# Forgetting attention with an FFN on one core: GpSimd scales the early exponentials and makes gl from the first group on

## The chip, the core and the metric

The kernel runs on one core of a Trainium2 chip. A core has five engines with an instruction queue each: TensorE (in the profile PE for matmuls and PEld for weight loads), VectorE (DVE), ScalarE (ACT), GpSimd (POOL) and SyncE (SP), which here only issues DMAs. Each works through its queue in order, and waits on semaphores where it needs another's result. The metric is the device time of one execution in microseconds. Before the change it is 1215.92 us, the median of three runs (1212.28 to 1219.12).

## The reference

Eight batches of eight heads, 576 tokens, head size 64. Attention has a forget gate: the logarithms of f are summed up along the sequence, and the difference of the sums at query and key is added to the scores. The result, 4608 tokens by 512, goes through an FFN with 2048 hidden units and a leaky ReLU.

```python
scores = scale * np.matmul(q, k.transpose(0, 1, 3, 2))
cum = np.cumsum(np.log(np.clip(f, 0.0001, 1.0)), axis=-1)
decay = cum[:, :, :, None] - cum[:, :, None, :]
scores = np.where(causal, -1000000000.0, scores + decay)
scores = scores - np.max(scores, axis=-1, keepdims=True)
attn = np.exp(scores)
attn = attn / (np.sum(attn, axis=-1, keepdims=True) + 1e-09)
x = np.matmul(attn, v)            # then rearranged to (4608, 512)
h = x @ w_in
g = np.maximum(0.01 * h, h)
out = g @ w_out
```

## The kernel before

**High and low halves.** The FFN's matmuls work on fp32r, in which a float32 is kept as a high half and a low half: x as xh and xl, the weights as win_h, win_l, wout_h, wout_l, the activations g as gh and gl. A product is the sum of three matmuls (high by high, high by low, low by high). The low half is always made by a subtraction, gl = g - gh.

**Early phase.** For the first three batches (NE = 3) the first 256 tokens are computed separately, two heads at a time: twelve steps, called pairs here. A pair (b, g) goes through

- `early_load`: DMAs of q, k (tile qk) and v (tile ve), issued by SP;
- `early_scores` (L254): score matmuls on TensorE (sce), eviction with mask and running extreme on DVE into four tiles ze (two of 128 x 128, two of 128 x 256; L279), exponentials on ACT with their sums into sume (L283), sume plus a small number and its reciprocal on DVE (L288, L289), and the scaling of the four ze by it (L291);
- `early_values`, one pair later: transposes of ze on TensorE (tre), their copies on ACT (pte, L303), the product with v (ave), and from it xh on ACT (L316) and xl on DVE (L317) for the FFN groups 0 and 1, or a copy xe that goes to DRAM (L312) for the third batch.

Between these, `weights` prepares sixteen pieces of weights (eight of w_in, eight of w_out, in turn): a DMA of 1 MB into one of two raw buffers (wraw), then two steps on ACT (wt at L170, the high half at L172) and five on DVE (L171, L173, L175, L179, and the low half at L180). All pieces go through one buffer wt.

**FFN.** `ffn` is a generator. A group is 256 tokens; a slice p of a group is 256 of the 2048 hidden units. For each slice TensorE makes h from 24 matmuls, ACT makes g (L587), DVE the high half gh (L590), and DVE or GpSimd the low half gl (L592). The second product (`second`, into o) of a slice is emitted one slice later, 24 matmuls. `fill(n)` takes n quanta of this generator; FQ says how many after each early pair (4 after the fifth, 8 after the sixth, then 8 after each).

**Main loop.** `for t in range(nt + 1)` (L675) works through 64 heads and pulls FFN quanta between their pieces; in its last round, t = nt, no new head is loaded. After it the FFN's rest is drained. In this loop GpSimd has work of its own: low halves of q and k (tiles s, m), of v (fixed_vs), of the groups' inputs (xs), and small copies. Before the loop it fills the fixed tiles (`fix`).

**Who makes gl.** `heads[0]` is False until the main loop begins, True for t < nt, and False again from t = nt on. Where it is True, GpSimd makes gl, else DVE. In the trace 111 are on GpSimd and 33 on DVE.

**Order.** The program is written in the order above, but a scheduler arranges the instructions anew by when it thinks that each can run, and fixes an order for each engine. So a change on one engine also moves instructions on others. A few matmuls on a tile of zeros (warm) stand among the early pairs to keep TensorE active.

Of the kernel before, what the change touches and what calls it, by code (L numbers as in the profile page):

```python
# [12 lines left out]
AF = mybir.ActivationFunctionType  # L13
ALU = mybir.AluOpType
# [23 lines left out]
def forgetting_attention_ffn(ctx, tc, qT, kT, v4, vr, f, w_in, w_out, out):  # L38
# [6 lines left out]
    nc = tc.nc  # L45
# [23 lines left out]
    def width(i):  # L69
        return min((i + 1) * P, S)  # L70
# [32 lines left out]
    def matmul(*args, **kw):  # L103
        work[0] += 1
        nc.tensor.matmul(*args, **kw)  # L105
# [7 lines left out]
    def warm(n):  # L113

        ps = psum.tile([P, 512], F32, tag="h", name=f"warm_{len(warmed)}")
        warmed.append(n)
        for _ in range(n):
            matmul(ps, still[:, :P], still, start=True, stop=True)
# [92 lines left out]
    for i in range(NCH):  # L211
        c = slice(i * P, width(i))
# [12 lines left out]
    def load(t):  # L225

        s, c0, c1 = tasks[t]
        h = state[t] = {}
        a, n = c0 * P, S
        for name, src, lo in (("q", qT, a), ("k", kT, 0)):  # L230
            x = h[name] = one.tile([P, S], F32, tag=f"{name}raw", name=f"{name}raw_{t}")
            for o in range(2):
                nc.sync.dma_start(x[o * D:(o + 1) * D, lo:n], src[s][:, lo:n])
        if s % 2 == 0:
            g = s // 2
            vm = fixed["vm"]
            nc.sync.dma_start(vm[:, :, :NFULL], v4[g])
            nc.sync.dma_start(vm[:REST, :, NFULL], vr[g])
            pairs[s // 2, c0] = {}
# [14 lines left out]
    def early_scores(b, g):  # L254
        e = early[b, g]
        mx = one.tile([P, 4], F32, tag="max", name=f"maxe_{b}_{g}", bufs=3)
        sm = one.tile([P, 4], F32, tag="sum", name=f"sume_{b}_{g}", bufs=3)
        for i in range(2):
            n = width(i)
            ps = [  # L260
                psum.tile([P, 512], F32, tag="sc", name=f"sce_{b}_{g}_{2 * o + i}")[:, :n]
                for o in range(2)
            ]
            for o in range(2):
                x = e["qk"][o * D:(o + 1) * D]
                matmul(ps[o], x[:, 0, i * P:n], x[:, 1, :n], start=True, stop=False)
            for o in range(2):
                s = b * HPB + 2 * g + o
                matmul(
                    ps[o], pick[:, s:s + 1].broadcast_to([P, P]), decay_r[i],  # L270
                    start=False, stop=True,
                )
            for o in range(2):
                c = 2 * o + i
                tag = ZE[g % 2][c]
                z = e[c] = one.tile(
                    [P, n], F32, tag=tag, name=f"ze_{b}_{g}_{c}", bufs=BUFS.get(tag, 1)
                )
                nc.vector.tensor_tensor_reduce(  # L279
                    out=z, in0=ps[o], in1=tri[:, TRI - n:], scale=-SCALE, scalar=3.0e38,  # L280
                    op0=ALU.add, op1=ALU.min, accum_out=mx[:, c:c + 1],
                )
                nc.scalar.activation(  # L283
                    z, z, AF.Exp, bias=mx[:, c:c + 1], scale=-1.0, accum_out=sm[:, c:c + 1]
                )
            if b * HPB // 2 + g < WARM[2]:
                warm(WARM[1])
        nc.vector.tensor_scalar(sm, sm, 1.0e-9, None, op0=ALU.add)  # L288
        nc.vector.reciprocal(sm, sm)  # L289
        for c in range(4):  # L290
            nc.scalar.activation(e[c], e[c], AF.Copy, scale=sm[:, c:c + 1])  # L291

    def early_values(b, g):
        e = early[b, g]
# [236 lines left out]
    def spans(t):  # L531
        a, n = tasks[t][1] * P, S
        return [(a, n)] if n - a <= 512 else [(a + P, n), (a, a + P)]

    groups, staged = {}, {}
    since, done = {}, []
# [7 lines left out]
    def fetch_group(n):  # L544
        if n not in groups and n not in staged and (n + 1) * T <= ready[0]:
            xs = staged[n] = one.tile([P, NCC, T], F32R, tag="b4", name=f"xs_{n}", bufs=B4)
            since[n] = work[0]
            nc.sync.dma_start(xs.bitcast(F32), xd[:, n * T:(n + 1) * T].rearrange("(c p) t -> p c t", p=P))
# [8 lines left out]
    def ffn():  # L557
        pending = None
        half = NFC // 2
        order = [(0, 0, HP), (1, 0, HP), (0, HP, half), (1, HP, half)]  # L560
        order += [(n, 0, half) for n in range(2, NG)]
        for at, (n, p0, p1) in enumerate(order):
            while (n + 1) * T > ready[0]:
                yield False
            if n not in groups:
                if n not in staged:
                    fetch_group(n)
                while n not in groups:
                    yield False
            acc = [None, None]  # L570
            for p in range(p0, p1):
                while len(loaded) < 2 * (p + 1):
                    yield False
                xh, xl = groups[n]
                ph = psum.tile([P, 2, T], F32, tag="h", name=f"h_{n}_{p}")
                for e in range(2):
                    fs = slice(e * P, (e + 1) * P)
                    for c in range(NCC):
                        for x, (w, xx) in enumerate(((win_h[p], xh), (win_h[p], xl), (win_l[p], xh))):
                            matmul(  # L580
                                ph[:, e, :], w[:, c, fs], xx[:, c, :],
                                start=(c == 0 and x == 0), stop=(c == NCC - 1 and x == 2),
                            )
                    if e == 0:
                        yield True
                g = one.tile([P, 2, T], F32, tag="b2", name=f"g_{n}_{p}", bufs=B2)
                nc.scalar.activation(g, ph, AF.Prelu, alpha=0.01)  # L587
                gh = one.tile([P, 2, T], F32R, tag="b2", name=f"gh_{n}_{p}", bufs=B2)
                gl = one.tile([P, 2, T], F32R, tag="b2", name=f"gl_{n}_{p}", bufs=B2)
                nc.vector.tensor_copy(gh, g)  # L590
                eng = nc.gpsimd if heads[0] else nc.vector
                eng.tensor_tensor(gl, g, gh.bitcast(F32), op=ALU.subtract)  # L592
                yield True
                if pending is not None:
                    yield from second(*pending)
                if p0 < p and at + 1 < len(order):
                    fetch_group(order[at + 1][0])
                pending = (n, p, p0, p1, gh, gl, acc)
        yield from second(*pending)
# [27 lines left out]

    parts = {}
    quanta = ffn()
    heads = [False]  # L630
    ready, used, credit = [0], [0], [0.0]

    def fill(n):

        settle()
        credit[0] += n
        while credit[0] >= 1:
            credit[0] -= 1
            if not next(quanta, None):
                credit[0] = 0  # L640
                return
            used[0] += 1

    nt = len(tasks)
# [28 lines left out]
    load(0)  # L673
    split(0)
    for t in range(nt + 1):  # L675
        heads[0] = t < nt
        if t + 1 < nt:
            load(t + 1)
        before = list(range(max(tasks[t - 1][1] - 1, 0), NCH)) if t else []
        now = list(range(*tasks[t][1:])) if t < nt else []  # L680
        have = ready[0] // T * NQ - used[0]
        left = min((e + 2 - t for e in ends if e + 1 >= t), default=1)
        step = min(have / (left + SLACK), MAXQ) / 8
        fill(step)
        for i in range(5):
            if i in before:
                transposes(t - 1, i)
            if i in now:
                scores(t, i)
            fill(step)  # L690
            if i == 1 and t and tasks[t - 1][0] % 2:
                inverse(t - 1)
        if t:
            for part in range(len(spans(t - 1))):
                values(t - 1, part)
                fill(step)
            if tasks[t - 1][0] % 2:
                normalise(t - 1)
            s, c0, c1 = tasks[t - 1]
            if s % HPB == HPB - 1:  # L700
                ready[0] = place[s // HPB, c0 * P] + S - c0 * P
        if t + 1 < nt:
            split(t + 1)
        fill(step * (3 - len(spans(t - 1)) if t else 1))
# [37 lines left out]
```

## Time and profile before

| | |
|---|---|
| median of three runs | 1215.92 us |
| the profiled execution's own time | 1216.96 us |
| its span, first to last instruction | 1215.0 us |
| PE busy | 1190.4 us (98%) |
| DVE busy | 623.4 us (51%) |
| ACT busy | 628.6 us (52%) |
| POOL busy | 467.9 us (39%) |
| L291 on ACT, 48 instructions | 17.9 us, 447 ns each |
| gl on POOL, 111 | 146.9 us, 1324 ns each |
| gl on DVE, 33 | 23.3 us, 705 ns each |

The span is cut into stages: the early phase runs to about 165 us, the main loop from there to about 1110 us, and the rest is FFN alone. A share of the whole span says little here; the stages differ. In rows of single instructions the first number is the start in microseconds from the span's begin, the second the duration; then engine, line, operation, output<-input with the program's names, shapes and count. A bracket at the end gives the idle time of the engine before it and what ended it. Durations of matmuls include their pipeline, so that TensorE's pace is read from rows with many of them.

### The profile page before, as it was taken

Reading aid. Unit: us, or ns where it says so; the run is one execution under the profiler, and the core shown is the slowest. Engines: PE = TensorE matmul, PEld = TensorE weight load, DVE = VectorE, ACT = ScalarE, POOL = GpSimd, SP = SyncE. Lnnn points to the kernel's source line nnn. Section 1 sums busy time; section 2 is a strip of 40 time slices with the busy share of each in tenths; the row PEclk is TensorE's granted clock in tenths of the full one; section 3 lists DMA queues with packets and bytes.
Section 4 is the critical chain, followed back from the end, with each engine's and each line's share of the span. In section 5 each row is a group of like instructions: output and inputs, shape, how many; then the busy total and the mean of one; then the engine's idle time right before and its main releaser. Section 6 shows DMA issues by size and latency. Waiting matters only on the chain.

```text
span 1215.0 us, 22228 instructions
## 1 busy us (share of the span) xinstructions
PE 1190.4 (98%) x7812; PEld 1070.4 (88%) x7812; DVE 623.4 (51%) x1682; ACT 628.6 (52%) x1631; POOL 467.9 (39%) x475
## 2 busy tenths in 40 slices
PE   8999989999999999999999999999999999999998
PEld 5678879888889999999999999999999999999997
DVE  6898556666645555455544444545444434553211
ACT  5876546667645565555545445454444444652111
POOL 2000255564455445454344453534454544531000
PEclk9899999999999999999999999999999999999999
DMA  6554233334333233323231322222223222211000
GB/s 193 168 192 165 83 103 110 95 104 140 107 106 97 79 97 97 114 80 92 83 109 51 89 80 90 73 90 61 75 84 90 60 69 81 72 57 47 18 18 18
DMA packets 81103, 110.53 MB, mean 91 GB/s; under 512 B 19616, under 2 KB 50704, under 8 KB 80992
## 3 DMA queue, kind: packets, MB, share of 16 engines
q1 hardware_dynamic: 80992, 109.11, 29.6%
q8 instruction: 62, 1.02, 0.3%
q14 instruction: 49, 0.40, 0.1%
HBM read 82.62 MB, written 18.58 MB: 83 GB/s over the span
## 4 chain that ended last, share of the span: by engine, by line
PE 86%; DVE 4%; ACT 3%; DMA 3%; issue 2%; POOL 1%; SPq 0%; ACTq 0%; POOLq 0%; DVEq 0%
PE h L105 32%; PE o L105 30%; PE tr L109 7%; PE av L105 7%; PE sc L105 7%; PE sce L105 1%; DMA kraw<-in_kT 1%; DMA wraw<-in_w_out 1%; ACT fixed_z L384 1%; PE ave L105 1%; DVE fixed_z L378 1%; DMA wraw<-in_w_in 1%; DVE pl L430 1%; DMA xd<-x 0%; DVE wraw L179 0%
## 5 line engine op out<-in xcount | busy, mean ns | idle before, releaser
L105 PE MATMUL h<-xh,win_h 128*128 128x256 f32 x1152 | 330.2, 287 | 0.3 <-ACT xh L316 0.3
L105 PE MATMUL h<-xh,win_l 128*128 128x256 f32 x1152 | 327.9, 285 | 0.0
L105 PE MATMUL h<-xs,win_h 128*128 128x256 f32 x1024 | 290.0, 283 | 4.0 <-POOL xs L143 4.0
L592 POOL TENSOR_TENSOR gl<-g,gh 128x512 fp32r<-128x512 f32 x111 | 146.9, 1324 | 290.9 <-DVE gh L590 269.0
L105 PE MATMUL o<-wout_h,gh 128*128 128x512 f32 x576 | 230.6, 400 | 0.0
L105 PE MATMUL o<-wout_l,gh 128*128 128x512 f32 x576 | 226.6, 393 | 0.0
L105 PE MATMUL o<-wout_h,gl 128*128 128x512 f32 x576 | 225.3, 392 | 0.0
L105 PEld LDWEIGHTS h<-xh,win_h 128*128 128x128 f32 x1152 | 220.7, 192 | 3.4 <-ACT xh L316 0.8
L105 PEld LDWEIGHTS h<-xh,win_l 128*128 128x128 f32 x1152 | 221.2, 192 | 0.7 <-issue 0.7
L384 ACT ACTIVATE fixed_z<-fixed_z,max 128x192 f32<-128x192 f32 (+3 forms) x272 | 161.0, 592 | 106.0 <-DVE max L378 102.4
L378 DVE CUSTOM_DVE_ANT_0 fixed_z<-sc,tri 128x192 f32<-128x192 f32 (+3 forms) x272 | 122.6, 452 | 159.3 <-PE sc L105 156.3
L105 PEld LDWEIGHTS h<-xs,win_h 128*128 128x128 f32 x1024 | 195.6, 191 | 6.6 <-POOL xs L143 4.6
L587 ACT ACTIVATE g<-h 128x512 f32<-128x512 f32 x144 | 85.8, 596 | 217.3 <-PE h L105 212.5
L428 ACT CAST ph<-tr 128x192 fp32r<-128x192 f32 (+3 forms) x360 | 126.4, 373 | 138.5 <-PE tr L109 98.6
L590 DVE CAST gh<-g 128x512 fp32r<-128x512 f32 x144 | 72.3, 502 | 209.4 <-ACT g L587 206.7
L430 DVE TENSOR_TENSOR pl<-tr,ph 128x384 fp32r<-128x384 f32 (+3 forms) x296 | 137.8, 467 | 76.2 <-ACT ph L428 75.7
L143 POOL TENSOR_TENSOR s<-qraw,s 64x576 fp32r<-64x576 f32 (+1 forms) x64 | 78.6, 1228 | 208.5 <-ACT s L347 208.5
L109 PE MATMUL tr<-ident_r,fixed_z 128*128 128x128 f32 x888 | 145.8, 274 | 7.3 <-DVE ph L435 2.4
L109 PEld LDWEIGHTS tr<-ident_r,fixed_z 128*128 128x128 f32 x888 | 107.4, 140 | 30.0 <-ACT rbr L508 5.0
L105 PEld LDWEIGHTS o<-wout_h,gl 128*128 128x128 f32 x576 | 108.2, 188 | 24.1 <-DVE maxe L279 0.4
L105 PEld LDWEIGHTS o<-wout_h,gh 128*128 128x128 f32 x576 | 108.7, 189 | 15.6 <-issue 0.3
L105 PEld LDWEIGHTS o<-wout_l,gh 128*128 128x128 f32 x576 | 108.8, 189 | 14.7
(108 smaller groups left out, 1731.9 us busy)
## 6 DMA issues: line engine op xcount, KB each, us to landing
kraw<-in_kT SPq DMA_DIRECT2D x128, 144.0 KB
qraw<-in_qT SPq DMA_DIRECT2D x80, 144.0 KB
wraw<-in_w_in SPq DMA_DIRECT2D x16, 512.0 KB
wraw<-in_w_out SPq DMA_DIRECT2D x16, 512.0 KB
fixed_vm<-in_v SPq DMA_DIRECT2D x32, 256.0 KB
xs<-xd SPq DMA_DIRECT2D x16, 512.0 KB
out<-ost SPq DMA_DIRECT2D x28, 256.0 KB
xd<-x SPq DMA_DIRECT2D x20, 288.0 KB
```

What stands on the lines that cost most here:

```text
L105: nc.tensor.matmul(*args, **kw)
L109: nc.tensor.transpose(*args)
L143: nc.gpsimd.tensor_tensor(out, a, b, op=ALU.subtract)
L378: nc.vector.tensor_tensor_reduce(out=z[:, a:b], in0=ps[:m, :b - a], in1=tri[:m, at:at + b - a], scale=-SCALE, scalar=3.0e38 if x == 0 else ...
L384: nc.scalar.activation(z, z, AF.Exp, bias=h["max"][:m, last:last + 1], scale=-1.0, accum_out=fixed["sum" + "ab"[s // 2 % 2]][:m, i, s % 2: ...
L428: nc.scalar.copy(strided(ph, run), source(ps, run))
L430: nc.vector.tensor_tensor(strided(pl, run), source(ps, run), strided(ph, run).bitcast(F32), op=ALU.subtract)
L587: nc.scalar.activation(g, ph, AF.Prelu, alpha=0.01)
L590: nc.vector.tensor_copy(gh, g)
L592: eng.tensor_tensor(gl, g, gh.bitcast(F32), op=ALU.subtract)
```

## The change

The scaling of the early exponentials goes from ACT to GpSimd, and gl is made by GpSimd in all cases but one: DVE makes it only after the main loop has ended (`done` is filled there). So fourteen gl of the early phase and one of the round t = nt move from DVE to GpSimd. What is computed stays the same.

```diff
         for c in range(4):
-            nc.scalar.activation(e[c], e[c], AF.Copy, scale=sm[:, c:c + 1])
+            nc.gpsimd.tensor_scalar(e[c], e[c], sm[:, c:c + 1], None, op0=ALU.mult)
...
-                eng = nc.gpsimd if heads[0] else nc.vector
+                eng = nc.vector if done else nc.gpsimd
                 eng.tensor_tensor(gl, g, gh.bitcast(F32), op=ALU.subtract)
...
-    heads = [False]
...
-        heads[0] = t < nt
```

The scheduler's orders change in the early phase, and at one place near the end. In the names of the rows below, the numbers behind a tile tell the pair within a batch, the slice or the buffer apart.

On ACT, before the change, ahead of the last xh of group 0 (the row of L316 with ave_3):

```order
L316 CAST xh_172<-ave_2_462 128x256
L283 ACTIVATE ze_0_1_499,sume_0_475<-ze_0_1_499,maxe_0_474 128x256
L283 ACTIVATE ze_0_3_502,sume_0_475<-ze_0_3_502,maxe_0_474 128x256
L170 ACTIVATE wt_519<-wraw_516 128x1024
L303 COPY pte_3_0_531<-tre_3_0_527 128x384
L303 COPY pte_3_1_537<-tre_3_1_533 128x384
L291 ACTIVATE ze_0_0_482<-ze_0_0_482,sume_0_475 128x128
L291 ACTIVATE ze_0_1_499<-ze_0_1_499,sume_0_475 128x256
L291 ACTIVATE ze_0_2_485<-ze_0_2_485,sume_0_475 128x128
L291 ACTIVATE ze_0_3_502<-ze_0_3_502,sume_0_475 128x256
L172 CAST win_h_95<-wt_519 128x1024
L316 CAST xh_172<-ave_3_539 128x256
```

The same place on ACT in the changed kernel:

```order
L316 CAST xh_172<-ave_2_462 128x256
L283 ACTIVATE ze_3_1_422,sume_3_398<-ze_3_1_422,maxe_3_397 128x256
L283 ACTIVATE ze_3_3_425,sume_3_398<-ze_3_3_425,maxe_3_397 128x256
L172 CAST wout_h_110<-wt_442 128x1024
L347 CAST s_1_1806<-qraw_1746 128x320
L283 ACTIVATE ze_0_0_482,sume_0_475<-ze_0_0_482,maxe_0_474 128x128
L303 COPY pte_3_0_531<-tre_3_0_527 128x384
L303 COPY pte_3_1_537<-tre_3_1_533 128x384
L283 ACTIVATE ze_0_2_485,sume_0_475<-ze_0_2_485,maxe_0_474 128x128
L170 ACTIVATE wt_519<-wraw_516 128x1024
L283 ACTIVATE ze_0_1_499,sume_0_475<-ze_0_1_499,maxe_0_474 128x256
L316 CAST xh_172<-ave_3_539 128x256
```

The scalings are gone, the cast of win_h_95 has moved behind the xh, and a cast of the main loop's first heads (s_1, with s_0 some rows earlier) has moved ahead of it. Its input qraw_1746 is loaded by SP ahead of the weight piece wraw_516, where before it stood two pieces later, and its buffer must first be left by s_0 on ACT and GpSimd.

On DVE, behind the same xh stands the last xl of group 0 (L317). Before:

```order
L171 TENSOR_SCALAR wt_519<-wt_519 128x1024
L279 ISA ze_1_2_624,maxe_1_613<-sce_1_2_616,tri 128x128
L279 ISA maxe_1_613 128x1
L173 TENSOR_SCALAR wraw_516<-wt_519 128x1024
L175 SCALAR_TENSOR_TENSOR wraw_516<-wraw_516 128x1024
L279 ISA ze_1_1_638,maxe_1_613<-sce_1_1_632,tri 128x256
L279 ISA maxe_1_613 128x1
L179 TENSOR_TENSOR wraw_516<-wt_519,win_h_95 128x1024
L317 TENSOR_TENSOR xl_173<-ave_3_539,xh_172 128x256
```

In the changed kernel:

```order
L171 TENSOR_SCALAR wt_519<-wt_519 128x1024
L317 TENSOR_TENSOR xl_173<-ave_3_539,xh_172 128x256
L288 TENSOR_SCALAR sume_0_475<-sume_0_475 128x4
L173 TENSOR_SCALAR wraw_516<-wt_519 128x1024
L289 RECIPROCAL sume_0_475<-sume_0_475 128x4
L279 ISA ze_1_0_621,maxe_1_613<-sce_1_0_615,tri 128x128
L279 ISA maxe_1_613 128x1
L175 SCALAR_TENSOR_TENSOR wraw_516<-wraw_516 128x1024
L279 ISA ze_1_2_624,maxe_1_613<-sce_1_2_616,tri 128x128
L279 ISA maxe_1_613 128x1
L179 TENSOR_TENSOR wraw_516<-wt_519,win_h_95 128x1024
```

Three weight steps (L173, L175, L179) and three evictions of the sixth pair, with the sixth pair's scores on TensorE, have moved behind the xl.

On TensorE, between the last scores of the eighth pair (sce_3) and its first transpose (tre_3), the changed kernel has ten o rows and two h rows behind the rest of ave_2; before, six transposes, eight o rows, the whole ave_2 and the ninth pair's scores stood there. The end of that stretch, before:

```order
L105 MATMUL sce_0_2_927<-both 128x128
L105 MATMUL h_0_997<-xh_174,win_h_93 128x256
L105 MATMUL h_0_997<-xl_175,win_h_93 128x256
L105 MATMUL sce_0_1_938<-qk_0_809 128x256
L105 MATMUL sce_0_3_939<-qk_0_809 128x256
L105 MATMUL sce_0_1_938<-both 128x256
L105 MATMUL sce_0_3_939<-both 128x256
L109 MATMUL tre_3_0_978<-ident_r,ze_3_0_822 128x128
```

In the changed kernel:

```order
L105 MATMUL o_1_0_692<-wout_l_119,gh_2_726 128x512
L105 MATMUL o_1_0_692<-wout_h_111,gl_2_727 128x512
L105 MATMUL h_0_997<-xh_174,win_h_93 128x256
L105 MATMUL h_0_997<-xl_175,win_h_93 128x256
L109 MATMUL tre_3_0_978<-ident_r,ze_3_0_822 128x128
```

The ninth pair's scores have moved behind the transposes. In the seventh pair, four o rows and the eighth pair's scores are likewise no longer ahead of the first transpose (tre_2), behind 22 h rows in both orders. On GpSimd the 48 scalings and nearly all early gl stand in the queue ahead of the main loop's work, with the low halves of s_0 and s_1 between them.

## The prediction

> **What bounds the kernel now.** I read the busy shares, then busy time by stage, then the chain of waits, then the rows of single engines where the chain leaves TensorE. By stage (start and end, length, then busy time and instructions of PE, PEld, DVE, ACT and POOL, granted clock, DMA share, GB/s):
>
> ```profile
> 17.00:53.00 36.00, 31.50 (x159) 21.49 (x156) 27.93 (x76) 29.90 (x87) 0.32 (x1) 0.86 0.59 187
> 53.00:75.00 22.00, 21.76 (x124) 17.65 (x124) 20.54 (x34) 13.51 (x28) 2.38 (x2) 0.92 0.52 177
> 75.00:137.00 62.00, 61.52 (x400) 50.15 (x401) 54.87 (x112) 45.94 (x109) 0.72 (x4) 1.00 0.50 162
> 380.00:1110.00 730.00, 728.72 (x4906) 669.95 (x4905) 346.64 (x997) 372.08 (x978) 327.77 (x321) 1.00 0.27 80
> ```
>
> From 53 us TensorE is busy practically all the time, so work taken from other engines there saves nothing unless TensorE waits for it. Only 17 to 53 us is slack: TensorE idles 4.5 us, its clock is 0.86, and ACT (29.90 of 36 us) and DVE (27.93) are the fullest. The chain (start, duration, what) alternates between ACT and DVE until TensorE starts on the first FFN group:
>
> ```profile
> 46.12 0.37 ACT xh L316
> 47.48 1.05 ACT wt L170
> 51.67 1.18 DVE wraw L179
> 52.85 0.34 DVE xl L317
> 53.23 5.10 PE h L105 x28
> 62.17 2.96 PE o L105 x12
> 65.13 2.87 PE h L105 x24
> ```
>
> The point to watch is the last xh and xl of group 0 (rows at 51.49 and 52.76 below): what brings them forward moves the dense stretch.
>
> **The scaling leaves ACT.** Twelve early pairs have four scalings each; a set takes 1.49 us of ACT:
>
> ```profile
> 49.16 1.49 ACT L291 ACTIVATE ze<-ze,sume 128x128 f32<-128x128 f32 x4
> 51.49 0.36 ACT L316 CAST xh<-ave 128x256 fp32r<-128x256 f32 x1
> 52.76 0.42 DVE L317 TENSOR_TENSOR xl<-ave,xh 128x256 fp32r<-128x256 f32 x1
> 54.47 0.44 ACT L347 CAST s<-qraw 128x320 fp32r<-128x320 f32 x1
> 49.37 0.70 DVE L173 TENSOR_SCALAR wraw<-wt 128x1024 int32<-128x1024 int32 x1
> ```
>
> Five sets stand ahead of the xh at 51.49: 5 x 1.49 = 7.5 us of ACT. By the order, two casts of s (2 x 0.44 us) move ahead of it and one cast of win_h (costed like the 1.05 us of the chain's wt row) moves behind it. ACT has about 7.6 us less to do before that xh.
>
> What GpSimd takes for it is not in the trace. The nearest rows are one-input work on few elements and two-input work on 320:
>
> ```profile
> L390 POOL COPY fixed_z<-fixed_z 64x64 f32<-64x64 f32 x64 | 16.9, 264 | 8.4 <-ACT fixed_z L384 8.0
> L654 POOL TENSOR_SCALAR_AFFINE_SELECT tri<-tri 128x128 f32<-128x128 f32 x1 | 0.3, 292 | 0.0
> L143 POOL TENSOR_TENSOR s<-qraw,s 64x320 fp32r<-64x320 f32 x24 | 21.5, 897 | 96.3 <-ACT s L347 96.3
> ```
>
> A set costs between 4 x 0.29 = 1.2 us and 4 x 0.90 = 3.6 us. I take 1.4 us (0.3 for 128 columns, 0.4 for 256), near the one-input rows, because the multiplication reads one tile. The Trainium skill's page "GPSIMD Engine Reference", section "3.1 Elementwise — side-by-side cycle accounting", puts such short loops at about 1.03 cycles per element, by my estimate 0.7 us a set plus dispatch; with that the sum below would end some 1 us lower.
>
> **GpSimd and DVE get in each other's way.** GpSimd is nearly idle here, but not free:
>
> ```profile
> 12.54 2.41 POOL L143 TENSOR_TENSOR fck<-fc,fck 64x576 fp32r<-64x576 f32 x1
> 14.92 2.40 POOL L143 TENSOR_TENSOR fcq<-start,fcq 64x576 fp32r<-64x576 f32 x1
> 150.94 1.45 POOL L143 TENSOR_TENSOR fixed_m2a<-kraw,m 64x576 fp32r<-64x576 f32 x1
> 13.77 2.27 DVE L179 TENSOR_TENSOR wraw<-wt,win_h 128x1024 f32<-128x1024 f32 x1
> 23.02 1.22 DVE L179 TENSOR_TENSOR wraw<-wt,wout_h 128x1024 f32<-128x1024 f32 x1
> 16.50 1.90 DVE L180 TENSOR_TENSOR win_l<-wraw 128x1024 fp32r<-128x1024 f32 x1
> 27.31 1.22 DVE L180 TENSOR_TENSOR wout_l<-wraw 128x1024 fp32r<-128x1024 f32 x1
> ```
>
> At 12 to 18 us the two run together: the GpSimd subtractions take 2.41 and 2.40 us where the same size takes 1.45 us at 151 us, and DVE's two weight steps take 2.27 and 1.90 us where they take 1.22 us with GpSimd idle. DVE loses 1.05 + 0.68 = 1.73 us to 2.9 us of GpSimd work: 0.6 us per us. The Trainium skill's page "SBUF — State Buffer", section "🔬 SBUF: two separate sides", speaks against this change: GpSimd and a DVE instruction with two SBUF inputs share a port pair, held exclusively for a whole instruction. These rows agree in kind; its full price is weighed among the rivals.
>
> Up to the xl at 52.76, five sets are 7.0 us of GpSimd; at 0.6 DVE loses 4.2 us, less what falls into its idle time (36.0 - 27.93 = 8.1 of 36 us, 22%): 3.3 us. In return the order puts three weight steps (L173 0.70 us and two costed at the 1.22 us of the rows above) and three score evictions (about 0.8 us, at some 0.3 us each) behind that xl: 3.9 us. DVE gains 0.6 us there, ACT 7.6 us. The chain alternates between the two, so the xl comes 0.6 to 7.6 us sooner; I take 4.0. But TensorE has also been given work behind that point: one set of 256-wide scores and three transposes.
>
> ```profile
> 79.78 1.06 PE sce L105 x6
> 80.84 0.66 PE tre L109 x6
> ```
>
> These cost 1.06 + 0.33 = 1.4 us. **Front: -4.0 + 1.4 = -2.6 us** (bounds -6.2 and +0.8).
>
> **What is late next.** The weights come next; the seventh piece is the tightest:
>
> ```profile
> 68.14 1.23 DVE L180 TENSOR_TENSOR win_l<-wraw 128x1024 fp32r<-128x1024 f32 x1
> 74.90 0.39 PE L105 MATMUL h<-xh,win_l 128*128 128x256 f32 x1
> 135.47 1.22 DVE L180 TENSOR_TENSOR wout_l<-wraw 128x1024 fp32r<-128x1024 f32 x1
> 151.08 2.75 PE o L105 x12
> ```
>
> It is ready at 69.4 and used at 74.9: 5.5 us to spare; the last piece has over 14 us (136.7 to 151.1). With TensorE 2.6 us sooner, 2.9 us are left. Until then DVE loses 0.6 x (6 sets of 1.4 us + 2 gl of 1.3 us) = 6.6 us, less a sixth in idle time, less two gl that it no longer makes (1.4 us): 4.1 us, if DVE alone sets the pace. So 1.2 us late at most, 0 if ACT's relief carries; I take **+0.5 us**.
>
> **Transposes wait for GpSimd.** In the seventh and eighth pairs the order now puts the first transpose closer behind the last scores: about 3.8 us of TensorE work between them (6.0 before) and 3.1 us (5.4 before), counted from the order at 0.12 us for an h row and 0.23 us for an o row (the chain rows of 24 and 12). Against that:
>
> ```profile
> 74.78 0.42 DVE L279 CUSTOM_DVE_ANT_0 ze<-sce,tri 128x256 f32<-128x256 f32 x1
> 75.28 1.17 ACT L170 ACTIVATE wt<-wraw 128x1024 f32<-128x1024 f32 x1
> 78.14 0.17 DVE L289 RECIPROCAL sume<-sume 128x4 f32<-128x4 f32 x1
> 79.22 1.49 ACT L291 ACTIVATE ze<-ze,sume 128x128 f32<-128x128 f32 x4
> ```
>
> Before, the path from last eviction to reciprocal took 3.5 us, 1.2 us of it ACT's weight step, which stood ahead of the exponentials and which the order now puts behind them. That leaves 2.3 us, then 0.7 us for two scalings on GpSimd: 3.0 us, plus up to one DVE instruction of 1.22 us. TensorE waits 0 to 0.4 us in one pair and 0 to 1.1 us in the other. I take **+0.7 us**.
>
> **gl on GpSimd.** Durations (minimum, median, maximum) of both forms:
>
> ```profile
> L592 POOL TENSOR_TENSOR gl<-g,gh x111: 1269/1289/2120, 165.0 to 1097.5; 128x512 fp32r<-128x512 f32 x111
> L592 DVE TENSOR_TENSOR gl<-g,gh x33: 681/691/1192, 58.5 to 1207.1; 128x512 fp32r<-128x512 f32 x33
> ```
>
> Fifteen move (fourteen early, one in the last loop round) and each takes 0.6 us longer. The second product that uses them stands one slice later, behind 24 h matmuls (2.87 us), and a gl on DVE queues behind weight steps of 1.22 us. I cost it at nothing; were that cover gone, each would cost 0.6 us, 9 us in all. The late one is hidden too: its successor on GpSimd starts after 12.18 us of idling.
>
> ```profile
> 1097.48 1.28 POOL L592 TENSOR_TENSOR gl<-g,gh 128x512 fp32r<-128x512 f32 x1 [3.67 <-DVE gh L590]
> 1110.94 2.38 POOL L143 TENSOR_TENSOR xs<-xs,xh 128x1024 fp32r<-128x1024 f32 x1 [12.18 <-DVE xh L553]
> ```
>
> **Sum.** -2.6 + 0.5 + 0.7 = -1.4 us. The profiled execution took 1216.96 us around a span of 1215.0, 1.0 us above the median of 1215.92; 1215.6 us by its clock is 1214.5 us by the median. That is my forecast.
>
> **Rivals.** (1) The two engines exclude each other fully and a set costs nearer to two-input work. At 1.0 us per us and 2.4 us a set, the front loses 12.0 x 0.78 = 9.4 us of DVE against the 3.9 moved: the xl is 5.5 us later, and the 1.4 us moved behind it are idle time. In the seventh and eighth pairs two scalings and a full DVE instruction make 2.3 + 1.2 + 1.2 = 4.7 us against 3.8 and 3.1: 0.9 + 1.6 us. 5.5 + 1.4 + 2.5 = 9.4 us slower: **1225.3 us**. It decides where DVE's loss before the xl passes 3.9 us by more than ACT's relief can use. For it: 2.27 us against 1.22. Against it: DVE lost 0.6, not 1.0, per us there. The lock of the SBUF page is this rival. (2) ACT alone sets the pace: xl 7.6 us sooner, nothing late behind it: 6.2 us faster, **1209.7 us**. Against it: DVE stands in the chain directly ahead of the first h. (3) The front gain goes to a new wait: the casts of s now stand on ACT ahead of xh, and the second needs a load that SP issues only once GpSimd has finished with the first s; the weight loads stand behind it on SP. That eats the 2.6 us, and 1.2 us of the later terms stay: **1217.1 us**. (4) The change does not do what it says: ruled out by the order, which shows all 48 scalings on GpSimd.
>
> **How the numbers follow.** Forecast 0.42, no gain (3) 0.26, slower (1) 0.18, faster (2) 0.14. A measurement of this kernel can tell about 0.5%, 6 us, from no change: below 1209.8 or above 1222.0. Rival (1) lies beyond it mostly, (2) about half: faster 0.10, same 0.73, slower 0.17. The range runs from 1209 to 1224: it takes in the front's bounds, (2), (3) and the nearer half of (1).
>
> **What would show it.** Right: the xl of group 0 and the first long run of h near 49 us instead of 53; POOL scalings of 0.3 to 0.4 us; DVE weight steps above 1.22 us where they meet GpSimd; waits of h for win_l and of tre for ze below 1.5 us; nothing changed after 170 us but a shift. Wrong: scalings of 0.8 us or more, DVE steps near 2 us throughout, the long run of h at 53 us or later, or ACT waiting for a load of q.

## The result, and the profile after

The changed kernel takes **1255.01 us** (median of four runs, 1253.49 to 1256.16) against 1215.05 us of the kernel before in the same session: ratio 1.0326, 95% interval 1.0302 to 1.0351, that is 39.6 us slower (0.0326 x 1215.05). The forecast was 1214.5 us with a range up to 1224.

From the page of the changed kernel, the busy times and the row of granted clocks (40 slices, tenths of full speed):

```profile
PE 1211.2 (97%) x7812; PEld 1079.4 (86%) x7812; DVE 620.3 (50%) x1667; ACT 614.4 (49%) x1583; POOL 548.0 (44%) x538
PEclk9687999999999999999999999999999999999999
```

The clock is lower only in slices 2 to 4, from 31 to 125 us. The windows say the same (width, busy us of PE, PEld, DVE, ACT, POOL, then clock, DMA share, GB/s):

```profile
17.00:53.00 36.00, 30.64 (x128) 19.21 (x129) 22.90 (x66) 19.66 (x52) 16.57 (x16) 0.81 0.50 156
53.00:75.00 22.00, 20.36 (x91) 15.21 (x92) 13.40 (x29) 11.37 (x27) 10.06 (x9) 0.69 0.30 104
75.00:137.00 62.00, 52.18 (x274) 38.36 (x273) 39.45 (x78) 27.57 (x62) 27.29 (x22) 0.83 0.40 132
380.00:1110.00 730.00, 725.25 (x4871) 666.98 (x4871) 347.59 (x1004) 377.16 (x993) 336.26 (x325) 1.00 0.29 85
```

ACT and DVE, the full engines of before, now have time to spare (11.37 and 13.40 us busy of 22), and TensorE gets through 274 matmuls between 75 and 137 us where it did 400. It idles 9.8 of those 62 us, and its clock is 0.83 instead of 1.00. All of the loss lies in the early heads: the transposes of the main loop (matmuls that write tr; median duration, first and last start) before,

```profile
L109 PE MATMUL tr<-ident_r,fixed_z x888: 270/272/417, 167.9 to 1100.4; 128*128 128x128 f32 x178
```

and in the changed kernel,

```profile
L109 PE MATMUL tr<-ident_r,fixed_z x888: 270/272/421, 205.0 to 1138.2; 128*128 128x128 f32 x178
```

start 37.1 us later and end 37.8 us later. The two spans differ by the same 37.8 us (1252.8 - 1215.0), and TensorE has the same number of matmuls ahead of the first tr in both. Behind it only 0.7 us was lost.

What TensorE waited for between 17 and 205 us (line waited for: us in all, times, longest), in the changed kernel:

```profile
PE tre L109 <- POOL ze L291: 10.7, 14, 1.5
PE sce L105 <- DVE maxe L279: 6.2, 2, 3.3
PE o L105 <- POOL gl L592: 4.9, 2, 3.9
```

Before, TensorE never waited for L291. The groups of scalings in the changed kernel, by form (busy us, mean ns of one, idle time before them):

```profile
L291 POOL TENSOR_SCALAR ze<-ze,sume 128x128 f32<-128x128 f32 x24 | 29.3, 1219 | 46.6 <-DVE sume L289 34.9 <-ACT wout_h L172 6.6 <-DVE maxe L279 5.1
L291 POOL TENSOR_SCALAR ze<-ze,sume 128x256 f32<-128x256 f32 x24 | 32.4, 1350 | 0.0
```

Its timeline around the fifth set, with VectorE's weight steps and some of the transposes, and then its last set (start, duration, what; a group of x4 includes the gaps in it):

```profile
49.52 1.22 DVE L175 SCALAR_TENSOR_TENSOR wraw<-wraw 128x1024 f32<-128x1024 uint32 x1
49.59 5.85 POOL L291 TENSOR_SCALAR ze<-ze,sume 128x128 f32<-128x128 f32 x4 [6.62 <-ACT wout_h L172]
50.86 1.22 DVE L179 TENSOR_TENSOR wraw<-wt,wout_h 128x1024 f32<-128x1024 f32 x1
52.92 1.22 DVE L180 TENSOR_TENSOR wout_l<-wraw 128x1024 fp32r<-128x1024 f32 x1
52.93 0.44 PE L109 MATMUL tre<-ident_r,ze 128*128 128x128 f32 x2 [0.40 <-POOL ze L291]
54.59 0.47 PE L109 MATMUL tre<-ident_r,ze 128*128 128x128 f32 x1 [1.22 <-POOL ze L291]
55.49 0.69 PE L109 MATMUL tre<-ident_r,ze 128*128 128x128 f32 x2 [0.43 <-POOL ze L291]
...
172.72 3.00 POOL L291 TENSOR_SCALAR ze<-ze,sume 128x128 f32<-128x128 f32 x4
```

The last set, which has no weight step beside it, takes 3.00 us: 0.60 us for each 128-column tile and 0.92 us for each of 256. The set at 49.59 lies beside three weight steps of VectorE and takes 5.85 us, while each of those steps keeps its 1.22 us. The transposes start as each tile comes out. The chain of waits then shows the dense stretch put off:

```profile
51.19 4.25 POOL ze L291 x3
55.49 0.69 PE tre L109 x2
...
62.10 5.83 PE h L105 x28
```

The first long run of h starts at 62.10 us; before it was 53.23.

### The profile page after: what moved, and what is told of

It reads as the page before. It is cut to its first block, busy times and chain, and to the rows that moved or that the text cites. A ratio compares the mean times of both kernels' runs of the same rounds, so it can differ in the third digit from the quotient of the medians.

```text
span 1252.8 us, 22270 instructions
## 1 busy us (share of the span) xinstructions
PE 1211.2 (97%) x7812; PEld 1079.4 (86%) x7812; DVE 620.3 (50%) x1667; ACT 614.4 (49%) x1583; POOL 548.0 (44%) x538
## 4 chain that ended last, share of the span: by engine, by line
PE 84%; DVE 5%; POOL 4%; ACT 3%; DMA 2%; issue 2%; SPq 0%; POOLq 0%; ACTq 0%; DVEq 0%
PE h L105 31%; PE o L105 29%; PE av L105 7%; PE tr L109 7%; PE sc L105 6%; POOL ze L291 2%; PE sce L105 1%; PE ave L105 1%; DMA wraw<-in_w_out 1%; DMA kraw<-in_kT 1%; ACT fixed_z L384 1%; DVE wraw L175 1%; POOL gl L592 1%; DVE wraw L179 1%; DVE fixed_z L378 1%
## 5 line engine op out<-in xcount | busy, mean ns | idle before, releaser
L592 POOL TENSOR_TENSOR gl<-g,gh 128x512 fp32r<-128x512 f32 x126 | 169.2, 1343 | 339.0 <-DVE gh L590 284.1
L105 PE MATMUL o<-wout_h,gl 128*128 128x512 f32 x576 | 227.9, 396 | 4.9 <-POOL gl L592 4.9
```

## The experiments

Three theories. **T1**: the scaling on GpSimd costs: by its own duration (T1a), because GpSimd is held up by VectorE's weight steps (T1b), or because the new order puts the transposes too close (T1c). **T2**: gl on GpSimd from the first group on costs: by a b2 buffer kept longer, for which SP waits (T2a), by gl's duration or the order (T2b), or by meeting VectorE's steps (T2c). **T3**: the one gl of the last round, costed at nothing. Losses are (ratio - 1) x 1215 us; pairs are counted from 0 here. The kernels of the experiments have other line numbers behind the edited places, so that the scaling is L283 or L288 in some of them. The scheduler gives each of them an order of its own; no run holds the order fixed.

### Which half of the change

e1 takes the scaling alone (the first added line in place of the removed one), e2 gl alone (the last pair of lines); e3 scales on VectorE (the second added line), and e4 leaves the scaling out.

```diff
-            nc.scalar.activation(e[c], e[c], AF.Copy, scale=sm[:, c:c + 1])
+            nc.gpsimd.tensor_scalar(e[c], e[c], sm[:, c:c + 1], None, op0=ALU.mult)
+            nc.vector.tensor_scalar(e[c], e[c], sm[:, c:c + 1], None, op0=ALU.mult)
-                eng = nc.gpsimd if heads[0] else nc.vector
+                eng = nc.vector if done else nc.gpsimd
```

> Only the scaling goes to GpSimd; gl stays as before. T1 (the sets of four scalings are the cause: 3.0 us alone and 3.2 to 7.5 us beside DVE's weight steps, against 1.49 us on ScalarE, with the transposes right behind): 1245 to 1256 us, nearly all of the 40 us, sets of 3.0 to 7.5 us as in the changed kernel. T2 (the early gl on GpSimd, queued behind the sets, is the larger part): below 1235 us.

> Only gl goes to GpSimd from the first group on; the scaling stays on ScalarE. T1: 1212 to 1222 us, no difference that can be told, since with no sets of scalings on GpSimd a gl waits there for nothing longer than 1.3 us. T2: over 1230 us.

> The scaling goes to VectorE, gl as before. T1 (it is GpSimd's duration that costs): a set costs 0.7 to 1.2 us, less than ScalarE's 1.49, but adds some 10 us to VectorE in the early heads: 1208 to 1222 us. T1c (any move of the scaling away from ScalarE lets the order put the transposes too close, whatever the engine's speed): over 1230 us.

> The kernel before with the scaling of the early heads' exponentials left out (their rows are not normalised). It bounds from above what the change could have won by relieving ScalarE of 18 us and the transposes of a wait of 1.49 us. T1 and T2 alike: 1203 to 1213 us, that is 3 to 12 us faster than before. If it is no faster than before, there was nothing to win by moving the scaling anywhere.

Measured: e1 1238.9 us, ratio 1.0197 (1.0153 to 1.0242), 23.9 us lost; e2 1223.7 us, 1.0072 (1.0050 to 1.0094), 8.7 us lost; e3 1223.75 us, 1.0070 (1.0046 to 1.0094); e4 1216.3 us, 1.0012 (0.9991 to 1.0032). So the scaling is the larger part, though less than T1 said (1245 us or more), and gl is not free as T1 said. 23.9 + 8.7 = 32.6 us: 7.0 us appear only when both are there (the three intervals, added as squares, leave some 7 us either way). In e1 TensorE waits for the scalings as in the whole change, and for no half of a weight:

```profile
PE tre L109 <- POOL ze L291: 11.0, 14, 1.5
```

e4 missed its expectation and is the plainest of these: with the scaling left out altogether the kernel is not faster, so moving it could win nothing that these runs can tell. In e3 a set takes about 1.0 us on VectorE from first start to last end (an instruction 0.28 to 0.35 us), less than the 1.49 us on ScalarE, and still 8.5 us are lost, between what T1 and T1c expected. TensorE waited for these scalings once, 0.5 us, so that wait is not the reason. The changed order or VectorE's extra work may be; neither was tested.

### GpSimd beside VectorE's weight steps

f1 is the kernel before, and f2 to f4 are e1, e2 and the whole change, all without the steps that make the low halves of the weights (the products take the high half in their place, so that TensorE has as many matmuls):

```diff
-        nc.vector.tensor_scalar(hi, t, -0x800000, None, op0=ALU.bitwise_and)
-        rest = lo.bitcast(F32)
-        nc.vector.scalar_tensor_tensor(
-            rest, lo.bitcast(U32), 2.0**-52, hi.bitcast(F32), op0=ALU.mult, op1=ALU.mult
-        )
-        hi = hi.bitcast(F32)
-        nc.vector.tensor_tensor(hi, tf, wh.bitcast(F32), op=ALU.subtract)
-        nc.vector.tensor_tensor(wl, hi, rest, op=ALU.add)
...
-     ((win_h[p], xh), (win_h[p], xl), (win_l[p], xh))
+     ((win_h[p], xh), (win_h[p], xl), (win_h[p], xh))
...
-     ((gh, wout_h[p]), (gh, wout_l[p]), (gl, wout_h[p]))
+     ((gh, wout_h[p]), (gh, wout_h[p]), (gl, wout_h[p]))
```

> The kernel before without the low halves of the weights: VectorE's four steps on each piece (L173, L175, L179, L180) are left out and the products that used a low half use the high half, so TensorE has as many matmuls as before. It is the base for the next run. Every theory: faster than before, 1195 to 1210 us.

> As the run without the low halves, but with the scaling on GpSimd (gl as before). VectorE no longer runs 1.22 us steps beside the scalings. T1a (a set of 3.0 us by itself, against 1.49, is what costs): 12 us or more slower than the run without the low halves. T1b (GpSimd waiting for VectorE's long steps, sets of 3.7 to 7.5 us, is what costs): sets of 3.0 to 3.6 us and at most 6 us slower than that run.

> gl on GpSimd from the first group on, scaling on ScalarE, without the low halves of the weights (low-half products use the high half). T2c (gl on GpSimd costs because it meets VectorE's 1.22 us steps): within 4 us of the base without low halves, 1213 to 1222 us. T2b (gl's own 1.29 us or the changed order costs): 6 to 12 us slower than the base.

> The whole change without the low halves of the weights. If what the scaling and gl lose together is lost to VectorE's long steps: within 5 us of the base without low halves (1217.6). If the two crowd each other out on GpSimd (gl behind a set, a set behind gl): 8 us or more slower than the base, since that does not need VectorE.

Measured: f1 1217.57 us, 1.0012 (0.9994 to 1.0031); f2 1214.77 us, 0.9984 (0.9967 to 1.0001); f3 1219.03 us, 1.0027 (1.0011 to 1.0044); f4 1221.31 us, 1.0055 (1.0031 to 1.0078). Against f1, the scaling on GpSimd loses nothing (3.4 us less, where e1 lost 23.9), gl loses 1.8 us (8.7), both together 5.2 us (39.6). The sets of f2 take 3.0 to 3.7 us, and TensorE hardly waits for them:

```profile
PE tre L109 <- POOL ze L283: 0.6, 2, 0.4
```

f1 missed: it is no faster than before, though VectorE is relieved of four steps on each of 16 pieces. VectorE's total work did not bound the early heads. f4 leaves 5.2 - (1.8 - 3.4) = 6.8 us that neither part has alone (some 5 us either way), about the 7.0 us above, and TensorE waits 3.9 us for the scalings where it waited 0.6 us in f2; so that share does not seem to need VectorE. Against its own expectation f4 is undecided: 5.2 us lie between the "within 5" of one theory and the "8 or more" of crowding. Crowding on GpSimd would look like this piece of the chain of the changed kernel, where gl stands behind the last scaling of a set:

```profile
76.15 1.99 POOL ze L291 x2
...
79.31 1.67 POOL ze L291
80.98 1.76 POOL gl L592
```

In f2 VectorE also has time to spare, which may hide a 3.0 us set. k5 to k7 part the two: on top of the edit of f1, in place of the four steps VectorE runs four maxima that read one SBUF tile.

```diff
+        for x in range(4):
+            nc.vector.tensor_reduce(
+                one.tile([P, 1], F32, tag="low", name=f"low_{n}_{x}", bufs=2), tf,
+                op=ALU.max, axis=mybir.AxisListType.X,
+            )
```

k6 has them in the kernel before, k5 in e1, k7 in e2.

> Scaling on GpSimd (gl as before); the low halves of the weights are left out, and in their place VectorE runs four maxima over 128x1024 per piece, reads of one SBUF tile that write one column, of about 1.1 us each, so that it is as busy as with the steps left out. If such reads don't hold GpSimd up, this parts the two readings of the pair without low halves: if GpSimd's waiting is the cause, sets stay at 3.0 to 3.7 us and the time is 1212 to 1223 us; if it is VectorE's being busy, sets of 3.0 to 3.7 us and yet 1228 us or more. If the reads hold GpSimd up too: sets of 4 us and more, over 1228 us, and the two stay unparted.

> The base of the run with the maxima: the same maxima of 1.21 us in place of the low-half steps, scaling on ScalarE, gl as before. If a set of 3.0 us by itself costs when VectorE is busy: 1213 to 1220 us, so that the run with the scaling on GpSimd (1230.3) is some 13 us slower than its base, and GpSimd's waiting accounts only for the rest of the 24. If the maxima themselves slow the kernel (four of 1.21 us are 0.5 us more than the steps they stand for, 8 us in all): 1224 us or more, and the 3.0 us sets cost at most 6.

> The maxima in place of the low-half steps, scaling on ScalarE, gl on GpSimd from the first group on. gl then takes its 1.29 us beside a busy VectorE that does not hold GpSimd up. If gl lost its 9 us by waiting for VectorE: within 4 us of the base with maxima. If by VectorE's being busy, by gl's own 1.29 us or by the order: 6 to 12 us slower than it.

Measured: k6 1219.54 us, 1.0044 (1.0029 to 1.0060); k5 1230.31 us, 1.0094 (1.0064 to 1.0124); k7 1220.79 us, 1.0049 (1.0025 to 1.0074). From the timeline of k5, a maximum and a set beside it:

```profile
46.02 1.19 DVE L174 TENSOR_REDUCE low<-wt 128x1 f32<-128x1024 f32 x1
46.28 2.99 POOL L288 TENSOR_SCALAR ze<-ze,sume 128x128 f32<-128x128 f32 x4 [1.62 <-DVE sume L286]
```

and what its transposes waited for:

```profile
PE tre L109 <- POOL ze L288: 7.4, 10, 1.7
```

A maximum (1.21 us in the mean) is as long as a weight step, and GpSimd runs beside it as if alone. By itself k5 came out as its second reading, short sets and yet over 1228 us. But part of that is not the scaling's: the maxima alone, in k6, lose 0.44%. With VectorE as busy but not in GpSimd's way, the scaling costs 1.0094 - 1.0044 = 0.50%, 6 us by the ratios (their intervals, added as squares, allow 2 to 10; the two profiled spans differ by 10.9 us). The other 18 of e1's 24 us (some 11 to 25 with e1's own interval) go with the weight steps. What the weight steps do that the maxima don't is to hold GpSimd up; they also make the low halves late, but in e1 TensorE waited for none, which speaks against that path. That GpSimd's waiting is how the 18 us arise is the reading that fits, not one that a run shows by itself: the scheduler's order differs between e1 and k5 too. For gl the answer is clearer: k7 is within 0.1% of k6 (some 4 us either way), so its own longer 1.29 us and its place on GpSimd cost nothing that shows, and the 8.7 us go with VectorE's steps. Where they meet, each side loses. From the timeline of e2, two early gl:

```profile
57.43 2.21 POOL L592 TENSOR_TENSOR gl<-g,gh 128x512 fp32r<-128x512 f32 x1 [1.40 <-DVE sume L289]
105.94 2.32 POOL L592 TENSOR_TENSOR gl<-g,gh 128x512 fp32r<-128x512 f32 x1 [13.92 <-PE sce L105]
```

and, 1.82 us of it on its chain of waits, a weight step that took 1.90 us (1.22 us when alone):

```profile
91.29 1.82 DVE wout_l L180
```

In e2 TensorE's waits for the evictions (sce for maxe) are 5.3 us against 1.4 before; how some us of meetings become 8.7 was not traced step by step.

### The buffers behind gl

In e2 and in the changed kernel SP waited for gl with the loads of q and k (changed kernel, 17 to 205 us):

```profile
SPq L248 <- POOL gl L592: 18.6, 3, 6.9
```

Before, the same wait (for a gl on VectorE) was 2.5 us. g0 and g1 are the kernel before and e2 with the v tiles taken out of the b2 buffers:

```diff
-        v = e["v"] = one.tile([P, 2, T // P, D], F32, tag="b2", name=f"ve_{b}_{g}", bufs=B2)
+        v = e["v"] = one.tile([P, 2, T // P, D], F32, tag=("qraw", "y")[g % 2], name=f"ve_{b}_{g}")
```

> The kernel before with the early heads' v tiles in buffers of their own, so that q and k, g, gh and gl share the five b2 buffers alone. It is the base for the next run. 1208 to 1218 us: fewer waits of SP for a b2 buffer, little change in time.

> gl on GpSimd from the first group on, scaling on ScalarE, v tiles in buffers of their own. T2a (gl on GpSimd costs its 9 us because it holds a b2 buffer longer, SP waits for it with the load of q and k, and the weight loads stand behind that on SP): within 3 us of the kernel before with v in buffers of its own, and SP's waits for gl below 4 us in all. T2b (gl's duration or the changed order itself costs): again 6 to 12 us slower than that.

Measured: g0 1216.37 us, 1.0003 (0.9986 to 1.0019); g1 1227.82 us, 1.0101 (1.0085 to 1.0118). gl costs 11.9 us here, not less, although SP's wait for it with L248 is 7.5 us in g1 against 11.3 in e2. That wait is not below the 4 us that the test needed, so g1 alone does not exclude T2a. But what T2a says of the rest of the path is not seen either: between 17 and 178 us ScalarE waited 3.9 us in g1 for weight pieces to land, less than the 5.3 us of g0, and TensorE waited for no load. In f3 SP waited 8.4 us for gl with the same loads, and gl lost 1.8 us; in k7 it waited 1.5 us, and gl lost nothing. T2a is not borne out, but it is not excluded as a part of the loss.

### Which pairs, and what room does

k2 and k3 scale pairs 0 to 4 and pairs 5 to 11 on GpSimd. In h0, h1 and k1 the values of pairs 4 to 6 and 8 to 10 are traced behind the FFN work of their step:

```diff
+        late = x >= 5 and steps[x - 1][1] < HPB // 2 - 1
+        if late:
+            fill(FQ[x])
         if x:
             early_values(*steps[x - 1])
...
-        fill(FQ[x])
+        if not late:
+            fill(FQ[x])
```

> The kernel before, with the scaling of pairs 0 to 4 alone on GpSimd, which have no FFN work to put between a set and its transposes. If the loss is the sum of what each set makes its transposes wait: 8 to 14 us slower than before, 1223 to 1229 us. If it needs all pairs: below 1220 us.

> The kernel before, with the scaling of pairs 5 to 11 alone on GpSimd, values where they were. If the loss is the sum over the sets: 8 to 14 us slower than before, 1223 to 1229 us, and with the run of pairs 0 to 4 about the 24 us of all. Below 1220 us: the later pairs lose only when the earlier ones have lost already.

> The kernel before with the transposes and values of pairs 4 to 6 and 8 to 10 traced behind the FFN work of their step, not ahead of it, so that more TensorE work lies between a set of scalings and its transposes. It is the base for the next run: 1208 to 1222 us.

> The same late values with the scaling on GpSimd (gl as before). If the loss is the latency of a lengthened set in front of its transposes, more work between them hides it: at most 8 us slower than the late values with the scaling on ScalarE, against 24 us without that room; the first five pairs, whose place is not changed, still lose some. If the loss has another path (engines held up, loads late): 15 us or more slower.

> Late values (as the base with late values), the scaling on GpSimd only for pairs 5 to 11, which mostly have the room; pairs 0 to 4 scale on ScalarE. If the 14 us left of the loss with late values come from the first five pairs: within 6 us of the base with late values, 1214 to 1223 us. If not: 1225 us or more.

Measured: k2 1229.93 us, 1.0100 (1.0073 to 1.0128), 12.2 us lost by five pairs; k3 1225.81 us, 1.0060 (1.0032 to 1.0088), 7.3 us lost by seven; together 19.5 of e1's 23.9. h0 1216.55 us, 1.0004 (0.9986 to 1.0022); h1 1230.78 us, 1.0138 (1.0107 to 1.0169); k1 1218.98 us, 1.0024 (0.9997 to 1.0052). With room for most of them the seven later pairs lose 2.4 us (k1 against h0), without it 7.3; with some 3 to 4 us either way on each, that difference is not clear of noise. h1 expected at most 8 us over h0 and lost 16.3; 12.2 us (k2) is what pairs 0 to 4, of which only the last was given room, lose by themselves. The window of h0 up to 75 us, then those of h1 up to 75 us and behind it:

```profile
17.00:75.00 58.00, 55.59 (x293) 41.96 (x294) 49.34 (x115) 45.07 (x114) 2.06 (x2) 0.85 0.56 177
...
17.00:75.00 58.00, 51.38 (x223) 35.42 (x224) 37.04 (x95) 30.65 (x76) 25.19 (x23) 0.76 0.44 136
75.00:165.00 90.00, 87.11 (x546) 70.39 (x545) 70.32 (x136) 48.55 (x105) 40.11 (x40) 1.00 0.45 144
```

Up to 75 us h1 does 223 matmuls at a clock of 0.76 (h0: 293 at 0.85); behind that TensorE is 97% busy at full clock, although GpSimd's sets are as long as in e1. This fits a loss that arises where a lengthened set stands directly ahead of its transposes. That is T1c's condition too: the price is paid where the order leaves no room, and the runs do not part duration and distance. No run was faster than the kernel before beyond its interval.

Put together, of the 39.6 us some 18 go with scalings beside VectorE's weight steps, 6 with the longer sets themselves while VectorE is busy, 8.7 with gl beside the weight steps, and 7 appear only with both moves; each of these is uncertain by 3 to 7 us.

## Why the prediction failed

**"A set costs ... I take 1.4 us"** is the first step that failed. It measured 3.00 us with nothing beside it (0.60 and 0.92 us an instruction) and 3.2 to 7.5 us beside the weight steps, 61.7 us for the 48 instead of 17. The bound of 3.6 us, from two-input work on 320 columns, held for a set alone. Of the one-input rows that were chosen for their kind, one was a copy of 64 columns; the other, an affine select of 128 x 128 at 0.29 us, was as large as a small tile and still took half of what the scaling takes. 128 more columns cost 0.32 us here, not the 0.1 us of the forecast. The estimate from the Trainium skill's page "GPSIMD Engine Reference", section "3.1 Elementwise — side-by-side cycle accounting" (1.03 cycles per element, 0.7 us a set plus dispatch), lay further off than the 1.4 us, and no run here agrees with it.

**"DVE loses ... 0.6 us per us"** is the step that failed worse, by its direction. It took the price of a meeting from VectorE alone and left out what GpSimd loses, though the same rows had shown it (2.41 us where 1.45 us was due). In e1 the scalings take

```profile
L291 POOL TENSOR_SCALAR ze<-ze,sume 128x256 f32<-128x256 f32 x24 | 33.6, 1401 | 0.0
L291 POOL TENSOR_SCALAR ze<-ze,sume 128x128 f32<-128x128 f32 x24 | 27.6, 1149 | 80.4 <-DVE sume L289 59.8 <-DVE maxe L279 12.2 <-ACT wout_h L172 4.3
```

that is 24.7 us more than the 36.5 us of 48 undisturbed ones. Fitting each one's duration (above 0.60 or 0.92 us) to the time that it lay beside each VectorE line gives 0.55, 0.64 and 0.61 us lost per us beside L175, L179 and L180, 0.81 and 0.40 beside the one-input steps L171 and L173, and 0.06 beside the evictions L279. The three long steps on VectorE kept medians of 1.22 to 1.23 us in e1, at most 1.47. How GpSimd's 24.7 us become 23.9 us of the kernel was not traced step by step.

The Trainium skill's page "SBUF — State Buffer", section "🔬 SBUF: two separate sides", says that whichever of the two starts first holds the pair and the other waits. The first scaling of the set at 49.59 agrees: it began 0.07 us behind L175 and took 1.6 us in place of 0.60. But VectorE did not wait in its turn: L179 at 50.86 began before that scaling had ended, at about 51.2 us, and kept its 1.22 us. With gl both sides waited (2.21 and 1.90 us above). Beside the maxima of k5, which read one tile, GpSimd lost 0.01 us per us. Such maxima are not among what that page of the Trainium skill lists as taking the pair. The prediction cited the page and then charged its price to VectorE alone; here GpSimd paid most of it.

**Front (-2.6 us).** It expected the xl of group 0 4.0 us sooner; it ends at 60.2 us instead of 53.2, 7.0 us later, and the long run of h starts 8.9 us later. ScalarE was relieved (19.66 us busy of 36 against 29.90), but e4 shows that this relief is worth nothing measurable even when it is free. The five sets ahead cost 12.2 us (k2).

**Transposes waiting (+0.7 us).** Right in kind, too small, and placed only in the seventh and eighth pairs; TensorE waited 14 times, 10.7 us in all. The loss is larger than the waits. A lower granted clock goes with them: in the changed kernel 0.69 and 0.83 from 53 to 75 and from 75 to 137 us, where it was 0.92 and 1.00 before. Taken over the windows that would be 22 x 0.23 + 62 x 0.17 = 15.6 us of full speed out of 39.6; in e1, with 0.69 and 0.97, 22 x 0.23 + 62 x 0.03 = 6.9 us out of 23.9. These are estimates from the windows; no run isolated the clock's share.

**Weights (+0.5 us).** Weight steps came later with everything else, but TensorE waited for no half of a weight in the changed kernel; no run isolates the term.

**gl (0 us, 9 us "were that cover gone").** Its 0.6 us a piece is hidden, as said (k7), yet gl alone lost 8.7 us that go with its meeting VectorE's steps, which this term did not contain; both moves together lost 7 us more than their sum. **The late gl (0 us)** held: from the first tr on, the changed kernel lost 0.7 us.

Rival (1), 1225.3 us, had the right sign and named the right meeting of the two engines. It priced a set at 2.4 us and charged the exclusion to VectorE ahead of the xl and to two pairs behind it, 9.4 us in all; early and late pairs both pay (k2, k3), and mostly on GpSimd. Two of the four listed signs of "wrong" came out, scalings of 0.8 us and more and the long run of h later than 53 us; VectorE's steps near 2 us throughout and ScalarE waiting for a load of q did not.

## What to carry to other kernels

Before an operation moves to an idle engine, ask what the move can win at most: leaving the scaling out bounded it at nothing that can be measured. Then price the new engine by the dear end of what its nearest rows allow until a row of the same operation shows otherwise: here neither like kind nor like size gave the price. And price a shared resource from both engines' rows: the one that loses may be the one whose output is waited for. A longer step seems to cost where its reader stands right behind it, so ask of each place how much work lies between.

## What the runs showed of the hardware that was not expected

- A GpSimd tensor_scalar with one scalar per partition took 0.60 and 0.92 us for 128 and 256 columns, which as a line through these two is 0.28 us + 2.5 ns per column.
- Not every VectorE instruction holds GpSimd up: maxima that read one SBUF tile (1.21 us each) and evictions that read PSUM left its scalings at 0.60 and 0.92 us; steps with two SBUF inputs and the one-input shift L171 (0.69 us) did not. Most of the time lost at these meetings was GpSimd's: VectorE's long steps stayed at 1.47 us or less in e1.
- Four weight steps of VectorE on each of 16 pieces could be left out without a gain (f1, 1.0012), while TensorE's waits for GpSimd, some 16 us (10.7 + 4.9), went with a loss of 40 us.
